# Strassen's scheme for the output products of the last four blocks of an attention and mixture kernel

## The chip, the cores and the metric

The kernel runs on one core of a Trainium2 chip. Such a core has a matrix engine (TensorE, PE in the profile; its weight loads stand apart as PEld), a vector engine (VectorE, DVE), an engine for activations and copies (ScalarE, ACT), a general engine (GpSimd, POOL) and an engine that only issues transfers (SyncE, SP). Each works through its own instructions in order and waits on semaphores for the others. Sixteen DMA engines move data between DRAM and the on-chip memory SBUF; matrix products land in PSUM, eight banks of 512 fp32 values in each of 128 partitions.

The metric is the device time of one execution in microseconds (us).

## The reference

```python
def phi(x):
    proj = np.einsum('bhsd,df->bhsf', x, w_phi)
    proj = proj - np.max(np.abs(proj), axis=-1, keepdims=True)
    return np.concatenate([np.exp(proj), np.exp(-proj)], axis=-1)
q_p, k_p = (phi(q), phi(k))
kv = np.einsum('bhsf,bhsd->bhfd', k_p, v)
z = np.sum(k_p, axis=2)
attn = np.einsum('bhsf,bhfd->bhsd', q_p, kv) / (np.einsum('bhsf,bhf->bhs', q_p, z)[..., None] + 1e-06)
x = attn.transpose(0, 2, 1, 3).reshape(4608, 512)
gate = 1.0 / (1.0 + np.exp(-(x @ w_gate)))      # w_gate, w_val: 512 x 1536
return gate * (x @ w_val) @ w_out               # w_out: 1536 x 512
```

There are 8 batches, 8 heads, 576 positions, 64 features a head, 128 random features, and all values are fp32. This document is about the second half, the gated product of 4608 tokens.

## The kernel before

**Arithmetic.** A factor is split into a high part in the matrix engine's own fp32 form and a low part (the rest), and one product of a 128x128 block takes three matmuls: high by high, high by low, low by high. A matmul loads a 128x128 weight block and streams up to 512 columns past it.

**Blocks.** The 1536 hidden features are twelve blocks j of 128. The first four (j = 0 to 3) are computed during attention, in 9 chunks of 512 tokens, straightforwardly (`gate`, L914; `first_js`, whose output product is `mm_out`, L971); their part of the result goes to DRAM as `ys`. The last eight are four pairs: pairs 0 and 1 (j = 4 to 7) in a first pass over all tokens, pairs 2 and 3 (j = 8 to 11) in a second. Both passes are `pass_over` (L1294), and they run over 6 chunks `dc` of 768 tokens, two halves of 384 each.

**One chunk of a pass.** `x_blocks` (L1149) fetches the four blocks of x (features by tokens) from DRAM, makes the four sums T1 to T4 of Strassen's scheme, and splits each of the seven factors that the scheme uses (`XB`: 11, T2, T3, T1, 21, T4, 22) into high and low (ACT L1187, DVE L1191). `group` (L1216) makes one 256x768 product with seven block products instead of eight: 7 x 2 x 3 = 42 matmuls of 384 columns (L1229), and five additions on DVE (L1242). There are four groups a chunk: gate and value of each of two pairs. `gated` takes the sigmoid on ACT (L1267); `valued` multiplies (DVE L1280), copies the high part (ACT L1284) and subtracts for the low part (DVE L1288). Then the output product: for each of the chunk's six blocks T of 128 tokens, the hidden values are the weights and w_out streams past, 2 pairs x 2 blocks x 3 = 12 matmuls of 512 columns (L1311). `finish` (L1129) fetches the sum so far (L1134), adds it on DVE (L1139) and stores the new sum (L1143): the first pass reads `ys` and writes `yt`, the second reads `yt` and writes `out`.

**Weights.** `combine` (L1054) makes the seven Strassen sums of the weights of one pair's gate (m = 0) or value (m = 1); those of pairs 2 and 3 are made during the first pass and kept in DRAM (`gscr`), and so are the w_out blocks (`out_weight`, `wscr`), a chunk's worth at a time, in the first four chunks. `fetched` (L1111) brings them back.

**Order.** Nothing is ordered by hand. `Plan.run` (L179) is a list scheduler at build time: every operation has an engine, an estimated duration and a rank, and the engine takes, of what can start, the lowest rank; what it finds is the program's order on each engine, which does not change on the chip. Buffers are slots of rings (`Buf`, `Slot`); an operation whose ring is full is not ready. In the passes PE's groups have banks `r_a` (5) and the output products `r_g` (3); x has 14 slots `r_X`, exactly one chunk's; h has 8 slots `r_h`; the y that come back have 3 (`r_y1`). All transfers of the loop are issued by SP, in order.

Of the kernel before, what the change touches and what calls it, by code (L numbers as in the profile page):

```python
# [59 lines left out]
KEEP = 30.0  # L60

# [87 lines left out]
class Plan:  # L149
# [3 lines left out]
    NEAR = {"PE": 0.3, "DVE": 0.05, "ACT": 0.05, "SP": 0.0, "X": 0.0}  # L153
    SAME = {"PE": 0.0, "DVE": 0.12, "ACT": 0.13, "SP": 0.0, "X": 0.0}
    RATE = 0.26
# [23 lines left out]
    def run(self):  # L179
        free = dict.fromkeys(self.NEAR, 0.0)  # L180
        ready = {e: [] for e in free}
        mode, wire = None, 0.0
# [30 lines left out]
        while left:  # L213
# [24 lines left out]
            if o.eng == "SP":  # L238
                wire = max(wire, t) + o.lag * self.RATE ** -1 * 1e-6
                end = wire + 2.0  # L240
            else:
                end = t + o.busy + o.lag
            if o.eng == "PE":
                mode = o.mode[-1]
            for cells in o.opens:
                n = len(cells.free)
                cells.free, cells.taken = [end] * n, [False] * n
# [5 lines left out]
            for n in o.then:  # L253
                n.wait -= 1
                if n.eng != o.eng or o.eng == "SP":
                    at = end + n.slack
                else:
                    at = t + o.busy + self.SAME[o.eng]
# [9 lines left out]
def attention_moe(  # L268
# [18 lines left out]
    actx = ExitStack()  # L287
# [13 lines left out]
    def arena(where, name, size, dtype):  # L301
# [9 lines left out]
        return lambda start=0: Area(view, cells, start * 1024 // CELL)  # L311
# [11 lines left out]
    for hd in range(2):  # L323
# [5 lines left out]
    yscr = [dram.tile([4, P, DM], F32, tag=f"ys{c}", name=f"ys{c}") for c in range(NCH)]  # L329
    y2scr = [dram.tile([4, P, DM], F32, tag=f"yt{c}", name=f"yt{c}") for c in range(NCH)]  # L330
    wscr = [dram.tile([2, P, DM], F32, tag=f"wo{j}", name=f"wo{j}") for j in range(NJ)]
# [3 lines left out]
        for m in range(2)  # L335
# [6 lines left out]
    flat, more = arena(ff, "flat", 32 << 10, F32), arena("two", "more", FB, F32)  # L342
# [14 lines left out]
    r_wo = x.ring(8, DM)  # L357
    x = high()
    r_G = x.ring(8, 7 * 2 * P)
    r_stage = x.ring(2, 7 * 2 * P)  # L360
    r_swo = high(56).ring(7, DM)
    r_x7 = high(42).ring(2 * NC4, CW)
    r_sum = flat(20).ring(1, 2 * DM)
    r_tmp = flat(24).ring(1, 2 * HT)
    r_f = flat().ring(5, HT)
    x = more()
    r_tmp += x.ring(2, 2 * HT)
    r_f += x.ring(6, HT)
# [410 lines left out]
    def weigh(j, m, r, deep, wh, wl, ms, part, after=()):  # L779
        raw = Buf([r_raw], [P, 2 * DM])  # L780
        top = Buf([r_top], [P, DM])
# [185 lines left out]
    def mm_out(acc, t, hs, j, first, last):  # L967
        (hh, hl), (wh, wl) = hs, weights[j][1]
        ts = slice(t * P, t * P + P)
        for i, (a, w) in enumerate(((hh, wh), (hh, wl), (hl, wh))):  # L970
            nc.tensor.matmul(  # L971
                acc(), a()[:, ts], w(), start=first and i == 0, stop=last and i == 2
            )

    def first_js(c, r, step):
# [5 lines left out]
        for t in range(CW // P):  # L981
            acc, y = Buf(banks, [P, DM]), Buf([r_y], [P, DM])

            def go(t=t, acc=acc):
# [15 lines left out]
                256 << 10, lambda t=t, y=y: nc.sync.dma_start(yscr[c][t], y()),  # L1000
# [33 lines left out]
    def swap():  # L1034
        actx.close()
        stage["two"] = ctx.enter_context(tc.tile_pool(name="two", bufs=1, side="right"))

    last = plan.op("X", 0.0, 0.0, swap, after=closing)
    last.opens = [a().cells for a in (high, more)]
    for cells in last.opens:  # L1040
# [5 lines left out]
    names = ["11", "12", "S3", "22", "S1", "S2", "S4"]  # L1046
# [7 lines left out]
    def combine(n, m, r, rings, after):  # L1054
# [7 lines left out]
        for i, j in enumerate(pair(n)):  # L1062
            weigh(
                j, m, r + 3 * i, False, gh, gl,
                slice(2 * i * KH, 2 * (i + 1) * KH), i, after + combined[-1:],
# [8 lines left out]
            )  # L1074
        for o, a, b, op in (
            (3, 2, 3, ALU.add),
            (2, 0, 2, ALU.subtract),
            (0, 3, 0, ALU.subtract),
            (1, 1, 0, ALU.subtract),
# [8 lines left out]
        for o, i, part in ((4, 3, 2), (2, 2, 1), (5, 0, 3), (6, 1, 4)):  # L1088
# [35 lines left out]
    def out_weight(j, r, rings, after):  # L1124
        wh, wl = Buf(rings, [P, DM]), Buf(rings, [P, DM])
        weigh(j, 2, r, False, wh, wl, slice(0, DM), None, after)
        return wh, wl

    def finish(T, acc, src, mark, dst, dmark, r):  # L1129

        c, t = divmod(T, CW // P)
        y1, y = Buf([r_y1], [P, DM]), Buf([r_y], [P, DM])
        sp(
            256 << 10, lambda: nc.sync.dma_start(y1().bitcast(F32), src[c][t]),  # L1134
            [(mark[c], t)], [y1], r - 12.0, [done],
        )
        dve(
            DM,
            lambda: vec.tensor_tensor(y(), acc(), y1().bitcast(F32), op=ALU.add),  # L1139
            [acc, y1], [y], -90.0,  # L1140
        )
        sp(
            256 << 10, lambda: nc.sync.dma_start(dst(c, t), y()), [y],  # L1143
            [(dmark[c], t)] if dmark else [], r,
        )

    prior, taken, outs = [fed], [], []

    def x_blocks(dc, r):  # L1149

        at_ = {n: (Buf([r_X], [P, 2, HT]), Buf([r_X], [P, 2, HT])) for n in XB}
        tmp = [Buf([r_tmp], [P, 2, HT]) for _ in range(3)]
# [6 lines left out]
        def fetch(x, K, h):  # L1159
            t, e = dc * DC + h * HT, dc * DC + h * HT + HT  # L1160
            s = 0
            while t < e:
                c, o = divmod(t, CW)
                wd = min(CW - o, e - t)
# [6 lines left out]
                    [xmark[c]], [x], rank(), prior[-1:],  # L1171
                )
                t, s = t + wd, s + wd
# [10 lines left out]
        def split(n, src):  # L1184
# [10 lines left out]
            )  # L1195

# [19 lines left out]
    def group(weight, x, r):  # L1216

        gh, gl = weight
        a, b, c, d = (Buf([r_a], [P, CW]) for _ in range(4))
        t1, t2, t3 = (Buf([r_f], [P, HT]) for _ in range(3))  # L1220

        def product(o, i, w, xn, first, last):
            k, (xh, xl) = names.index(w) * KH, x[xn]

            def go():
                for cc in range(2):
                    ws = slice(k + cc * P, k + cc * P + P)
# [193 lines left out]
```

## Time and profile before

| what | value |
|---|---|
| median of 3 runs | 1159.23 us (1158.13 to 1159.84) |
| profiled execution, its own time | 1160.85 us |
| its span, first to last instruction | 1158.9 us |
| granted TensorE clock, mean | 0.998 |
| DRAM traffic | 120.06 MB read, 49.42 MB written |
| first matmul of the passes | 598.3 us after the span's start |
| last matmul of the passes ends | 1155.2 us |

The profile is of one execution, about 1.6 us over the median. "Busy" of an engine is the time in which an instruction of it stands in the trace; matmuls are pipelined and overlap, so a busy PE alone does not say that it runs at its pace: the number of matmuls in a stretch does. The chain of waits is followed back from the last instruction, and in order of time it shows, for every stretch, what was on it and how many. In the rows of groups the pair after the bar is total busy time in us and the mean in ns; behind the second bar stands how long the engine had been idle before these instructions.

### The profile page before, as it was taken

What the parts mean: (1) busy time and instruction counts of PE and PEld (TensorE: products, weight loads), DVE (VectorE), ACT (ScalarE), POOL (GpSimd) and SP (SyncE); (2) the same over time, 40 slices, a digit from 0 to 9 for tenths busy, and PEclk for the clock granted to TensorE, in tenths of its full rate; (3) what the DMA queues carried; (4) which work ended last, traced back from release to release, by engine and by line L of the source; (5) the groups of instructions that cost most, each with busy time, mean ns of one, the idle gap of its engine ahead of it and who ended that gap; (6) DMA issues with size and microseconds to landing.
All of it is one profiled execution on the core that took longest, in us unless ns stands there. A gap on an engine that the chain in (4) does not pass through costs nothing.

```text
span 1158.9 us, 22323 instructions
## 1 busy us (share of the span) xinstructions
PE 1142.8 (99%) x8796; PEld 939.5 (81%) x8796; DVE 933.3 (81%) x1793; ACT 583.0 (50%) x1115; POOL 0.7 (0%) x6
## 2 busy tenths in 40 slices
PE   8999999999999999999999999999999999999998
PEld 6666566766676677678889999999999999999997
DVE  6999989888878878847897999988767757757764
ACT  6867776666656666635553444352332333323421
POOL 0000000000000000000000000000000000000000
PEclk9999999999999999999999999999999999999999
DMA  6764554344424443226526656545447433225122
GB/s 237 226 220 127 152 168 123 121 129 137 137 87 153 121 137 122 70 79 209 173 101 211 206 178 223 187 141 186 154 173 286 141 106 123 78 88 163 56 95 82
DMA packets 99441, 171.08 MB, mean 148 GB/s; under 512 B 18825, under 2 KB 43529, under 8 KB 99337
## 3 DMA queue, kind: packets, MB, share of 16 engines
q1 hardware_dynamic: 99336, 169.66, 45.7%
q8 instruction: 69, 1.13, 0.4%
q14 instruction: 36, 0.29, 0.1%
HBM read 120.06 MB, written 49.42 MB: 146 GB/s over the span
## 4 chain that ended last, share of the span: by engine, by line
PE 84%; DVE 7%; DMA 6%; ACT 2%; issue 1%; SPq 1%; DVEq 0%
PE bank L1229 30%; PE gate L1311 17%; PE gate L914 11%; PE gate L971 6%; PE bank L621 4%; PE bank L663 3%; PE bank L914 3%; DMA rb<-den 3%; PE bank L432 2%; PE bank L681 2%; DMA den<-dn 2%; PE bank L537 1%; DVE d L587 1%; PE bank L971 1%; PE bank L635 1%; PE bank L647 1%
## 5 line engine op out<-in xcount | busy, mean ns | idle before, releaser
L1229 PE MATMUL bank<-low,high 128*128 128x384 f32 x2016 | 351.8, 336 | 0.0
L1229 PEld LDWEIGHTS bank<-low,high 128*128 128x128 f32 x2016 | 349.8, 188 | 1.1
L1311 PE MATMUL gate<-low 128*128 128x512 f32 x864 | 198.4, 389 | 0.0
L1311 PEld LDWEIGHTS gate<-low 128*128 128x128 f32 x864 | 162.0, 188 | 33.2
L914 PE MATMUL gate<-low 128*128 128x512 f32 x696 | 165.7, 393 | 1.2 <-ACT flat L949 0.6
L914 PEld LDWEIGHTS gate<-low 128*128 128x128 f32 x696 | 128.6, 188 | 29.7 <-issue 1.2
L479 ACT ACTIVATE ek<-ek 128x512 f32<-128x512 f32 (+1 forms) x192 | 96.6, 526 | 27.3 <-DVE ek L467 25.9
L1242 DVE TENSOR_TENSOR more<-more,bank 128x384 f32<-128x384 f32 x111 | 61.1, 551 | 40.8 <-PE bank L1229 40.3
L971 PE MATMUL gate<-low 128*128 128x512 f32 x384 | 92.3, 394 | 0.0
L971 PEld LDWEIGHTS gate<-low 128*128 128x128 f32 x384 | 70.8, 188 | 15.1 <-issue 1.0
L621 PE MATMUL bank<-ek,vin 128*32 128x256 f32 x1240 | 74.5, 386 | 4.4 <-ACT d L545 3.8
L621 PEld LDWEIGHTS bank<-ek,vin 128*32 128x32 f32 x1240 | 37.8, 110 | 46.2 <-issue 11.0
L1139 DVE TENSOR_TENSOR flat<-gate,low 128x512 f32<-128x512 f32 x72 | 49.3, 685 | 23.3 <-PE gate L1311 11.7
L438 DVE TENSOR_REDUCE mk<-bank 128x4 f32<-128x512 f32 (+1 forms) x92 | 49.0, 552 | 21.3 <-PE bank L432 16.9
L1242 DVE TENSOR_TENSOR flat<-flat,bank 128x384 f32<-128x384 f32 x75 | 41.3, 551 | 29.3 <-PE bank L1229 29.1
L1187 ACT CAST low<-more 128x768 fp32r<-128x768 f32 x36 | 30.1, 836 | 61.1 <-DVE more L1178 60.8
L467 DVE TENSOR_TENSOR ek<-bank,mk 128x512 f32<-128x512 f32 (+1 forms) x92 | 48.2, 550 | 0.6 <-ACT d L550 0.2
L1267 ACT ACTIVATE more<-more 128x384 f32<-128x384 f32 x38 | 20.0, 525 | 57.1 <-DVE more L1242 56.9
L938 ACT CAST low<-flat 128x512 fp32r<-128x512 f32 x36 | 22.3, 620 | 51.5 <-DVE flat L963 44.9
L1284 ACT CAST low<-more 128x384 fp32r<-128x384 f32 x50 | 24.7, 513 | 46.6 <-DVE more L1280 46.6
L590 ACT ACTIVATE eq<-d 128x1152 f32<-128x1152 f32 x29 | 33.9, 1168 | 24.8 <-DVE d L587 24.4
L432 PE MATMUL bank<-wk,kin 64*128 64x128 f32 x496 | 38.7, 289 | 4.6 <-DMA kin<-k 4.3
(184 smaller groups left out, 1700.1 us busy)
## 6 DMA issues: line engine op xcount, KB each, us to landing
flat<-w_moe SPq DMA_DIRECT2D x36, 512.0 KB
low<-xs SPq DMA_DIRECT2D x46, 256.0 KB
kin<-k SPq DMA_DIRECT2D x32, 320.0 KB
qin<-q SPq DMA_DIRECT2D x32, 320.0 KB
vin<-v SPq DMA_DIRECT2D x32, 320.0 KB
ys<-flat SPq DMA_DIRECT2D x36, 256.0 KB
low<-ys SPq DMA_DIRECT2D x36, 256.0 KB
yt<-flat SPq DMA_DIRECT2D x36, 256.0 KB
```

The lines of the kernel that those rows point to most:

```text
L432: nc.tensor.matmul(pk[hd]()[:, t, :], x()[head(hd), t * P : t * P + P], wk[head(hd), :], start=True, stop=True,)
L438: vec.tensor_reduce(mx, pk, axis=AX.X, op=ALU.max, apply_absolute_value=True)
L467: vec.tensor_tensor(ek[g]()[:, :, F:], src, mk[g]()[:, :ns].unsqueeze(2).broadcast_to([P, ns, F]), op=ALU.subtract,)
L479: lambda g=g, sg=sg: act.activation(ek[g]()[:, :, sg * F : sg * F + F], ek[g]()[:, :, F:], AF.Exp, scale=1.0 - 2.0 * sg,),
L621: nc.tensor.matmul(o_[o : o + Q, : 2 * F], vx()[:, 2 * t + hd, o % D : o % D + Q], (e0, e1)[hd][:, t, :] if t < 4 else e2[:, 0, :], start= ...
L663: nc.tensor.matmul(nm()[o : o + Q, :], w()[:, sg, o : o + Q], es[sg]()[:, o // D, cs], start=sg == 0, stop=sg == 1, tile_position=(0, o),)
L914: nc.tensor.matmul(o(), a()[:, ws], x(), start=cc + n == 0, stop=cc == NC4 - 1 and n == 2,)
L971: nc.tensor.matmul(acc(), a()[:, ts], w(), start=first and i == 0, stop=last and i == 2)
L1139: lambda: vec.tensor_tensor(y(), acc(), y1().bitcast(F32), op=ALU.add),
L1229: nc.tensor.matmul(o()[:, :HT], s()[:, ws], y()[:, cc, :], start=first and cc + i_ == 0, stop=cc + i_ == 3, skip_group_check=not first,)
L1242: lambda: vec.tensor_tensor(o(), p(), q()[:, :HT], op=ALU.add),
L1311: nc.tensor.matmul(acc(), s()[:, h, o : o + P], w(), start=i + e + k_ == 0, stop=i + e + k_ == 4,)
```

## The change

Five things are done together, for the two passes only.

1. **Outputs turned.** The output products give output features by tokens: w_out is now the weight and the hidden values stream (`mm_out`, `first_pass`). The kernel's result is 512 x 4608, and the host turns it; `ys` is laid out like x. In the first pass an output is 4 feature blocks x 2 token halves, each 12 matmuls of 384 columns. The first pass adds its result straight into `out`.
2. **Strassen for the output products of the second pass.** `combine` is also run for m = 2 (w_out of a pair), in the last two chunks of the first pass, in place of `out_weight`. `values` makes the seven Strassen sums of the hidden values (four subtractions), in two wide buffers, and splits them. `sent` is a group whose seven products sum over both pairs: 7 x 2 x 3 = 42 matmuls of 384 columns, twice a chunk (m = 0, 1).
3. **Sums of x kept.** The first pass stores T1 to T4, both parts, in DRAM (`tscr`; 8 stores of 384 KB a chunk, not for the last chunk, which is the first of the second pass and stays in SBUF). The second pass fetches them.
4. **Results added by accumulating transfers.** In the second pass GpSimd issues four transfers a `sent` that add to `out` in DRAM; only the last `sent` fetches, adds on DVE and stores through SP.
5. **Order and room.** The second pass takes chunk 5 first, then 0 to 4; the second half of chunk 5's first-pass outputs is put off into the second pass; gates of the next chunk stand between the two `sent` of a chunk; all eight banks serve both. `raw`, `top` and the weight sums of `combine` move to a region that is opened when attention ends, and that region later holds hidden sums (`third`). The planner's transfer rate is 0.36 instead of 0.26 after attention.

The diff, cut to its core:

```diff
-    def mm_out(acc, t, hs, j, first, last):
+    def mm_out(acc, m, hs, j, first, last):
...
-        for i, (a, w) in enumerate(((hh, wh), (hh, wl), (hl, wh))):
+        for i, (w, a) in enumerate(((wh, hh), (wh, hl), (wl, hh))):
             nc.tensor.matmul(
-                acc(), a()[:, ts], w(), start=first and i == 0, stop=last and i == 2
+                acc(), w()[:, ms], a(), start=first and i == 0, stop=last and i == 2
             )
...
+            if n in kinds and dc < NDC - 1:
+                for i, x in enumerate(at_[n]):
+                    k = 2 * kinds.index(n) + i
+                    sp(
+                        384 << 10, lambda k=k, x=x: nc.sync.dma_start(kept_x(k), flat_x(x)),
+                        [x], [(tmark[dc], k)], r + 8.0,
+                    )
...
+        if again:
+            for n in XB:
+                if n in kinds:
+                    for i, x in enumerate(at_[n]):
+                        k = 2 * kinds.index(n) + i
+                        sp(
+                            384 << 10,
+                            lambda k=k, x=x: nc.sync.dma_start(flat_x(x), kept_x(k)),
+                            [(tmark[dc], k)], [x], rank(), prior[-1:],
+                        )
+                else:
+                    fetch(at_[n][1], int(n[0]) - 1, int(n[1]) - 1)
+                    split(n, at_[n][1])
...
-    def group(weight, x, r):
+    def group(terms, r, banks, temps, names=names[0], plus=None):
...
+            for n, (weight, part) in enumerate(terms):
...
+                o_ = pe(
+                    "f", 1.05 / len(terms), go, [*weight, *bufs], [o],
+                    r + 1.04 * (i + n / len(terms)), 0.3, taken[-1:],
+                )
...
+    def first_pass(dc, r):
...
+        for T in range(2 * NC4):
+            acc = Buf([r_g], [P, CW])
+            h, m = divmod(T, NC4)
+            ro = r + 29.2 + 2.1 * T + (SPAN if h and dc == NDC - 1 else 0.0)
...
+    def values(n, x, v, r, banks, after):
+
+        g = group(on_x(ws[n, 1], x), r, banks, r_f2)
+        for i, src in zip((1, 3, 0, 2), g):
+            dve(
+                HT,
+                lambda i=i, src=src: vec.tensor_tensor(
+                    v()[:, i, :], v()[:, i, :], src()[:, :HT], op=ALU.mult
+                ),
+                [src], [(v, i)], -100.0,
+            )
...
+        less(of(t, 0), of(v, 2), of(v, 1), [(v, 2), (v, 1)], [t])
+        less(of(v, 2), of(v, 3), of(v, 2), [(v, 3)], [(v, 2)])
+        less(of(t, 1), of(v, 3), of(t, 0), [(v, 3)], [t])
+        less(of(t, 2), of(v, 0), of(t, 1), [(v, 0)], [t])
+        at_ = {}
+        for src, rings, width, kinds_ in (
+            (v, r_hA, 4, ("21", "11", "T3", "22")),
+            (t, r_hB, 3, ("T1", "T2", "T4")),
+        ):
+            hh, hl = (Buf([rings], [P, width, HT]) for _ in range(2))
+            on_act(
+                width * HT, lambda hh=hh, src=src: act.copy(hh(), src()), [src], [hh], -95.0,
+                after,
+            )
+            dve(
+                width * HT,
+                lambda hh=hh, hl=hl, src=src: vec.tensor_tensor(
+                    hl(), src(), hh().bitcast(F32), op=ALU.subtract
+                ),
+                [src, hh], [hl], -95.0, after=after,
+            )
...
+    def sent(ns, hs, dc, m, r, last=False):
...
+        a, t2, t3, t1 = group(
+            on_h([ws[n, 2] for n in ns], hs, m), r, both, r_f2, names[2], ys
+        )
...
+                plan.op(
+                    "POOL", 0.9, 192 << 10,
+                    lambda f=f, h=h, t=t: nc.gpsimd.dma_start(
+                        final(f, dc, h), t(), accum_op=ALU.add
+                    ),
+                    [t], to, r,
+                )
...
+    for n, dc in enumerate(turns):
+        banks, wait = (both, 0.0) if n else ([r_a], 8.4)
+        hs = [values(2, xb, gv, r, banks, [stored])]
+        gv = gates(3, xb, r + 7.3, banks)
+        hs.append(values(3, xb, gv, r + 14.6, banks, [summed]))
+        if n:
+            sent(ns, hs, dc, 0, r + 21.9)
+        if n < NDC - 1:
+            xb = x_blocks(turns[n + 1], r + 29.2 + wait - XLEAD, True)
+            gv = gates(2, xb, r + 29.2 + wait, both)
+        if not n:
+            r += 15.7
+            sent(ns, hs, dc, 0, r + 21.9)
+        sent(ns, hs, dc, 1, r + 36.5, n == NDC - 1)
+        r += PASS
```

More of the change, by code (lines that the diff above doesn't have):

```diff
@@ L334, in attention_moe @@
         for n in range(2, 4)
-        for m in range(2)
+        for m in range(3)
     }
@@ L341, in attention_moe @@
     low, high = arena(ff, "low", RA, F32R), arena("two", "high", RB, F32R)
-    flat, more = arena(ff, "flat", 32 << 10, F32), arena("two", "more", FB, F32)
+    flat, more = arena(ff, "flat", 32 << 10, F32), arena("prep", "more", FB, F32)
+    third = arena("three", "third", FB, F32R)
     x = low()
@@ L357, in attention_moe @@
     r_wo = x.ring(8, DM)
+    r_hA = low(48).ring(4, 4 * HT)
+    r_hB = low(42).ring(1, 3 * HT) + third().ring(3, 3 * HT)
+    r_O = low(72).ring(2, 7 * 2 * P)
     x = high()
@@ L777, in attend, with weigh @@
             t += wd
-    def weigh(j, m, r, deep, wh, wl, ms, part, after=()):
-        raw = Buf([r_raw], [P, 2 * DM])
-        top = Buf([r_top], [P, DM])
+    def weigh(j, m, r, deep, wh, wl, ms, part, after=(), again=False):
+        raw = Buf([r_raw2 if again else r_raw], [P, 2 * DM])
+        top = Buf([r_top2 if again else r_top], [P, DM])
         def words(x):
@@ L1151, in x_blocks @@
+    prior, taken, outs, sums = [fed], [], [], []
+    omark, tmark = ([Buf() for _ in range(NDC)] for _ in range(2))
+    kinds = ("T1", "T2", "T3", "T4")
+    def x_blocks(dc, r, again):
         at_ = {n: (Buf([r_X], [P, 2, HT]), Buf([r_X], [P, 2, HT])) for n in XB}
-        tmp = [Buf([r_tmp], [P, 2, HT]) for _ in range(3)]
+        tmp = [] if again else [Buf([r_tmp], [P, 2, HT]) for _ in range(3)]
         n_, since = [0.0], len(plan.ops)
@@ L1159, in fetch @@
         def fetch(x, K, h):
[L1160 to L1164, printed above, removed]
+            for c, o, s, wd in pieces(dc, h):
                 sp(
@@ L1251, in group @@
         add(t2, t1, c)
+        first = t1
+        if plus:
+            for o, p, q in ((t2, t2, plus[1]), (plus[2], t1, plus[2]), (t1, t1, plus[3])):
+                add(o, p, q)
+            first = plus[2]
         product(d, 3, "S1", "T1", True, False)
@@ L1327, in attention_moe, with gates @@
-    SPAN = 46.0
-    y2mark = [Buf() for _ in range(NCH)]
+            finish(m, dc, h, acc, ro)
+        return x
+    both = [r_a, r_g]
+    def gates(n, x, r, banks):
+        g = group(on_x(ws[n, 0], x), r, banks, r_f2)
+        v = Buf([r_V], [P, 4, HT])
+        for i, src in zip((1, 3, 0, 2), g):
+            on_act(
+                HT,
+                lambda i=i, src=src: act.activation(v()[:, i, :], src()[:, :HT], AF.Sigmoid),
+                [src], [(v, i)], -100.0, exps,
+            )
+        return v
@@ L1353, in attention_moe, with swap_again @@
+    stored = plan.op("X", 0.0, 0.0, lambda: None, after=plan.ops[-2:])
+    summed = plan.op("X", 0.0, 0.0, lambda: None, after=[stored, *sums])
+    def swap_again():
+        pctx.close()
+        stage["three"] = ctx.enter_context(tc.tile_pool(name="three", bufs=1, side="right"))
+    plan.op("X", 0.0, 0.0, swap_again, after=[stored]).opens = [third().cells]
     start += SPAN * NDC
-    for n, m, late in ((2, 0, []), (2, 1, taken[-4:-3]), (3, 0, outs[-8:-7]), (3, 1, outs[-1:])):
+    for n, m, late in (
+        (2, 0, []), (2, 1, taken[-4:-3]), (3, 0, outs[-12:-11]), (3, 1, outs[-12:-11]),
+    ):
@@ L1355, in attention_moe @@
         ws[n, m] = fetched([r_G], 7 * KH, gscr[n, m], marks[n, m], start, late)
-    for j in (*pair(2), *pair(3)):
-        wo[j] = fetched([r_wo], DM, wscr[j], marks[j], start + 10.0)
-    for dc in range(NDC):
-        pass_over((2, 3), dc, start + SPAN * dc, ws, wo, y2scr, y2mark, final, None)
+    for n in (2, 3):
+        ws[n, 2] = fetched([r_O], 7 * KH, gscr[n, 2], marks[n, 2], start + 20.0, [stored])
+    ns = 2, 3
+    turns = [NDC - 1, *range(NDC - 1)]
+    r = start + 7.3
+    gv = gates(2, xb, start, [r_a])
```

255 lines of the change are left out of this document (165 added, 90 removed).

## The prediction

> **What bounds the kernel now.** I began with the page: busy times, then the chain that ended last by engine.
>
> ```profile
> PE 1142.8 (99%) x8796; PEld 939.5 (81%) x8796; DVE 933.3 (81%) x1793; ACT 583.0 (50%) x1115; POOL 0.7 (0%) x6
> ...
> PE 84%; DVE 7%; DMA 6%; ACT 2%; issue 1%; SPq 1%; DVEq 0%
> ```
>
> PE stands busy nearly always and carries the chain. A busy PE need not run at its pace, so the next view is the chain in order of time (start, length, what, how many) over the second pass.
>
> ```profile
> 886.50 24.96 PE bank L1229 x144
> 911.46 16.36 PE gate L1311 x72
> 927.82 29.12 PE bank L1229 x168
> ...
> 1109.73 29.12 PE bank L1229 x168
> 1138.86 16.37 PE gate L1311 x72
> 1155.23 0.02 issue
> 1155.25 0.69 DVE flat L1139
> ```
>
> Every chunk has the same two lengths to a hundredth: 168 group products in 29.12 us, 72 output products in 16.36 us, nothing between. So PE waits for nothing here. A 384-column matmul takes 29.12/168 = 0.1733 us from start to start, a 512-column one 16.36/72 = 0.2272 us. That is 0.451 against 0.444 ns a column: a fixed part of some 0.012 us stands on each. In these passes a matmul less is time less, and any wait of PE is time more.
>
> Third, the same chunks by windows (busy of PE, PEld, DVE, ACT, POOL with instructions, clock, DMA share, GB/s): two of the first pass, one of the second, then two short stretches in which transfers crowd.
>
> ```profile
> 654.70:700.20 45.50, 45.50 (x241) 42.64 (x240) 44.97 (x87) 21.10 (x39) 0.00 (x0) 1.00 0.65 216
> ...
> 791.20:836.70 45.50, 45.50 (x242) 42.66 (x241) 36.92 (x66) 16.27 (x31) 0.00 (x0) 1.00 0.46 156
> ...
> 911.40:956.90 45.50, 45.50 (x242) 42.66 (x241) 31.97 (x54) 15.57 (x28) 0.00 (x0) 1.00 0.34 105
> ```
> ```profile
> 890.00:895.00 5.00, 5.00 (x30) 5.00 (x29) 2.49 (x6) 0.92 (x3) 0.00 (x0) 1.00 1.02 404
> 895.00:900.00 5.00, 5.00 (x30) 5.00 (x30) 4.37 (x10) 2.28 (x5) 0.00 (x0) 1.00 1.02 341
> ```
>
> DVE is nearly full in the first pass (combining weights) and has room in the second. Full DMA engines move 341 to 404 GB/s; the second pass uses 105.
>
> **PE's own time.** First pass: 72 x 512 columns become 96 x 384. 96 x 0.1733 = 16.64 for 16.36 us, +0.28 a chunk, **+1.7** for six. Second pass: 84 x 0.1733 = 14.56 for 16.36 us, -1.80 a chunk, **-10.8** for six. Net **-9.1 us**. The products of `mm_out` keep shape and count: 0. The form (128x128 weights, 384 columns) is that of L1229, so its pace is measured, and in the all-384 stretches above PEld is already at 5.00 of 5.00, so a saturated load row is within that pace.
>
> The Trainium skill ("TensorE: Matmul & The Clock Gate", section "Wait — 56ns, not 53.3ns?") gives a warm matmul N / 2.4 GHz and some 2.5 ns. By it 384 columns take 0.1625 and 512 0.2158 us, and the change would be worth 504 x 0.1625 + 576 x 0.1625 - 864 x 0.2158 = -11.0 us. The rows show a fixed part five times that, so the narrower matmuls keep less; the sum goes by the rows.
>
> **What is off PE.** Durations of the new shapes come from these groups (busy us, mean ns, idle before):
>
> ```profile
> L1242 DVE TENSOR_TENSOR more<-more,bank 128x384 f32<-128x384 f32 x111 | 61.1, 551 | 40.8 <-PE bank L1229 40.3
> ...
> L1139 DVE TENSOR_TENSOR flat<-gate,low 128x512 f32<-128x512 f32 x72 | 49.3, 685 | 23.3 <-PE gate L1311 11.7 <-DMA out<-flat 9.5 <-DMA yt<-flat 1.6
> ...
> L587 DVE TENSOR_TENSOR d<-d,mb 128x1152 f32<-128x1152 f32 x29 | 39.1, 1348 | 0.0
> ...
> L1191 DVE TENSOR_TENSOR low<-low 128x768 fp32r<-128x768 f32 x36 | 34.2, 950 | 0.1
> ...
> L1187 ACT CAST low<-more 128x768 fp32r<-128x768 f32 x36 | 30.1, 836 | 61.1 <-DVE more L1178 60.8
> ...
> L1288 DVE TENSOR_TENSOR low<-more,low 128x384 fp32r<-128x384 f32 x50 | 27.7, 554 | 5.1 <-ACT low L1284 4.0
> ...
> L1284 ACT CAST low<-more 128x384 fp32r<-128x384 f32 x50 | 24.7, 513 | 46.6 <-DVE more L1280 46.6
> ```
>
> DVE takes 0.398 us for each 384 columns more (950 to 1348 ns), ACT 0.323 (513 to 836). An estimate for 1536 columns is then 1.75 on DVE and 1.48 on ACT.
>
> *DVE, second pass, a chunk:* two groups more, 10 x 0.55 = +5.5; eight subtractions, +4.4; low parts 2 x (1.75 + 1.35) for 8 x 0.55, +1.8; x needs three splits for four sums and seven splits, -8 x 0.95 = -7.6; no `finish`, -6 x 0.685 = -4.1. Together 0: about 32 of 43.7 us. *DVE, first pass:* `out_weight` goes (six instructions of 0.42 to 0.69, -3.3), `finish` is 8 x 0.55 for 6 x 0.685 (+0.3), but combining runs in all six chunks, not four: 42 to 45 of 45.8 us throughout. PE covers it, as in the first chunk quoted; the last combined weights may come 10 us into the second pass, and are wanted 37 us in. ACT stays near 15 us a chunk. All at 0 while PE's products cover it; without that cover DVE's excess over 45.8 us would show directly.
>
> *Hidden sums, the new wait.* After the last value product of pair 3 (call its end V) stand in a row: one addition, one multiplication, two subtractions (4 x 0.55), ACT's wide copy (1.48), DVE's wide subtraction (1.75), with four hand-overs of some 0.1 to 0.2: about 6.0 us. `sent` comes next on PE in rank. Without pair 3 it can do the pair 2 half of four products, 4 x 3 x 0.1733 = 2.08 us. In the four middle chunks the next chunk's gates (42 x 0.1733 = 7.28 us) can stand in the hole: 9.4 against 6.0, hidden; I take 0.25 a chunk for hand-overs, +1.0 (0 to 15.7, if that filler fails: 4 x (6.0 - 2.08)). The last chunk has no next gates; it has both `sent`, 4.16 us of halves, against 6.0: **+1.9** (0 to 6.0). Behind PE's waiting product is everything on PE, and DVE behind it.
>
> *Between the passes* the same chain has one group as filler, and pair 3's w_out sums go where w_out lay, so they are fetched only after the put-off outputs: 1.84 MB at 341 to 404 GB/s is 4.5 to 5.4 us, and up to 3 us latency (the last store below, 2.96). Cover: 7.28 + 2.08 = 9.4. It fits narrowly: +1.0 (0 to 7.3, if the gates are not there).
>
> *Transfers of x.* The second pass fetches 11 x 384 KB = 4.33 MB a chunk instead of four blocks, into slots that the last group frees from V - 6.2 on. At 341 GB/s that is 12.7 us; with 2.3 us latency and the last split (0.84 + 0.95) the last block is ready at V + 10.6. PE, filling 14.6 us with gates and `sent`, wants it at V + 13.5. Cover holds down to 4.33 MB / 15.6 us = 277 GB/s. SP waits there for PE, as now:
>
> ```profile
> SPq L1167 <- PE bank L1229: 90.8, 11, 20.9
> ```
>
> and behind it queue only this x, since the results leave through POOL.
> *First pass:* stores of T1 to T4 add 3.15 MB a chunk, `out_weight` takes 1.05 away: 216 + 2.1 MB / 45.5 us = 262 GB/s, below 341. 0, with the rival below.
>
> *Accumulating transfers.* The page shows POOL with 6 instructions and no transfer of the loop. 44 transfers of 192 KB; the nearest row is a plain 256 KB store by SP at the end: DVE ends at 1155.94, the span at 1158.9, so 2.96 us. Between that and twice that (reading the target too), 3 to 6 us, I take 4. They hold temporaries of a ring of nine: two `sent` take eight, the next group's first the ninth, and its second must find one of the earlier eight free again, some 10 us after the first `sent` ended. Nothing is late until a transfer holds its buffer that long: 0 (up to 5 a chunk beyond it).
> The Trainium skill ("DMA: Bandwidth & Descriptors", "Anatomy of one DMA — SWDGE (gpsimd) path") puts a GpSimd transfer at 2.0 us and bytes / 436 GB/s, an estimate of 2.45 us here, accumulation not counted. That lies under what I took; no row of this trace shows it.
>
> *Ends.* After the last product 0.55 for 0.69 on DVE and 64 KB less: -0.3. At the front, `combine` can fetch raw weights only once attention's room is free; they are needed when the first groups start, and until then old products fill PE. 0, or up to 5 us if that filler ran out.
>
> **Sum.** -9.1 + 1.0 + 1.9 + 1.0 - 0.3 = -5.5. The profiled execution took 1160.85 us (span 1158.9 and 1.95 around it): 1155.3. The median shown is 1159.23: **1153.7 us**. About 0.2% (2.3 us) is what a measurement can tell from no change: 1156.9 to 1161.5 counts as the same.
>
> **Rivals.**
> *The hole stays open (slower).* Each middle chunk's gates wait for x, so the chain of 6.0 us stands bare after 2.08 us of halves. Wholly: 15.7 + 1.9 + 4 at the turn - 9.4 = +12.2, 1171.4; with half of the middle holes (7.85) +4.4, 1163.6. It decides from 277 GB/s downwards, or where the release-to-landing time grows by 3 us. For it: x has exactly one chunk's slots, and fetch, split, group and chain meet in 15 us. Against it: mean traffic there would be (4.33 + 1.57 to 3.1 MB) / 43.7 us = 135 to 170 GB/s. Chance 0.17.
> *First pass pays for the stores.* The old results come back into three buffers, now wanted every 2.08 us instead of 2.73, with stores of 1 us each (384 KB at 400 GB/s) ahead in the same engines. One output in eight late by 1 us is 6 us: 1159 to 1160, the same. For it: 262 GB/s mean, in bursts. Against it: no wait at 216. Chance 0.12.
> *Transfers of POOL hold buffers or SBUF over 10 us.* 1157 to 1165. Chance 0.05, both halves alike.
> *The change does less than it says* would be a 384-column output at more than 0.1733 us; L1229 excludes it.
>
> **Chances.** Forecast, 1149.8 (no waits) to 1156.9: 0.66. With a little of the rivals on either side: faster 0.67, same 0.15, slower 0.18. The range reaches from no waits to half the open holes: 1149.8 to 1163.6.
>
> **What would show it.** Right: in the chain, 96 first-pass outputs in 16.64 us, 42 products of a `sent` in 7.28, and chunks of the second pass 43.7 us apart; PE idle only after the last values (about 2 us) and at the turn. Wrong: gaps before `sent` in each chunk released by DVE or ACT (hole), by a transfer of x (supply); first-pass chunks longer than 45.8 us (stores); additions waiting for POOL's transfers.

## The result, and the profile after

The changed kernel took **1169.36 us** (median of 9 runs, 1163.14 to 1172.34), the kernel before 1159.99 us on the same chips (9 runs): ratio **1.0067, 95% interval 1.0044 to 1.009**. It is slower by 9.4 us where 5.5 less were forecast, and lies above the range. The profiled execution, the longest of the nine, took 1172.34 us (span 1170.5), 17.0 more than the 1155.3 that the sum gave for such an execution.

The page of the changed kernel, busy times and the chain by engine:

```profile
PE 1142.5 (98%) x9012; PEld 966.3 (83%) x9012; DVE 951.3 (81%) x1826; ACT 585.6 (50%) x1095; POOL 39.2 (3%) x50
...
PE 47%; issue 19%; DVE 16%; DMA 9%; ACT 4%; POOL 3%; SPq 1%; DVEq 0%; POOLq 0%; ACTq 0%
```

PE's busy time is what it was (it is a model, and hides pace), yet PE's share of the chain fell from 84% to 47%. Part of that is only the view's: over most of the second pass the chain follows GpSimd's queue (POOL and "issue", pieces of up to 31.87 us), while PE was busy for 257.61 of 259 us. In order of time the chain shows that the products themselves run at the forecast pace:

```profile
791.91 13.54 PE gate L1407 x78
...
888.84 29.12 PE bank L1286 x168
917.96 7.30 PE gate L1407 x42
925.26 1.06 PE bank L1286 x6
```

78 output matmuls of the first pass in 13.54 us are 0.1736 us each; a `sent` takes 7.3 us. The third view counts matmuls in a stretch (us, busy of PE, PEld, DVE, ACT, POOL with instructions, clock, DMA share, GB/s):

```profile
600.00:880.00 280.00, 273.11 (x1538) 268.02 (x1537) 245.21 (x462) 115.17 (x216) 0.00 (x0) 0.99 0.67 233
...
889.00:1148.00 259.00, 257.61 (x1476) 255.60 (x1475) 183.47 (x303) 83.46 (x129) 34.95 (x40) 1.00 0.57 144
...
1145.00:1166.00 21.00, 18.35 (x102) 17.14 (x101) 15.18 (x25) 3.97 (x5) 3.53 (x4) 1.00 0.31 47
```

The yardsticks: the first experiment below has the same products in the same order without first-pass waits, and holds 1598 in 600 to 880. So 60 are missing here, 60 x 0.1733 = 10.4 us; a wait of 1.55 us at the window's start (602.8 to 604.3) belongs to the front. The second pass has one shape; 259 us hold 1494 and 21 us hold 121. Missing are 18 (3.1 us) and 19 (3.3 us).

Without the front, the first pass is the stretch from the first to the last of its 576 output matmuls; of the changed kernel, then of the first experiment:

```profile
L1407 PE MATMUL gate<-low x576: 333/334/444, 642.6 to 927.0; 128*128 128x384 f32 x192
```
```profile
L1407 PE MATMUL gate<-low x576: 334/334/372, 638.3 to 914.3; 128*128 128x384 f32 x192
```

That is 284.4 us for 276.0: the first pass pays **8.4 us**.

*Where the first pass loses it.* Waits of DVE and PE in 598 to 889 (total us, times, longest), then the chain through its first output stretch:

```profile
DVE flat L1168 <- DMA low<-ys: 8.5, 9, 1.9
...
PE bank L1286 <- DVE flat L1305: 5.3, 5, 2.2
```
```profile
652.73 4.20 DMA low<-ys
...
660.02 0.43 SPq L1161
...
660.50 5.14 DMA low<-ys
...
665.74 0.10 DVE flat L1168
...
666.62 0.47 DVE flat L1305
...
667.23 4.93 PE bank L1286 x18
```

An old result, at most 192 KB, is fetched (`low<-ys`) and lands 5.14 us later. DVE's next instruction is the addition that wants it (L1168, `finish`), and DVE works in order, so a group's addition (L1305) stands behind it; that addition would have freed a bank, and PE starts again at 667.23 after 2.24 us. The windows say what the transfers met:

```profile
645.00:650.00 5.00, 5.00 (x30) 4.81 (x28) 4.82 (x10) 3.41 (x7) 0.00 (x0) 1.00 0.20 79
650.00:655.00 5.00, 5.00 (x29) 4.87 (x29) 5.00 (x9) 0.51 (x2) 0.00 (x0) 1.00 0.93 311
655.00:660.00 5.00, 5.00 (x31) 5.00 (x30) 4.58 (x7) 0.82 (x1) 0.00 (x0) 1.00 0.94 330
660.00:665.00 5.00, 4.99 (x29) 4.67 (x27) 3.60 (x8) 1.21 (x3) 0.00 (x0) 1.00 0.90 303
...
680.00:685.00 5.00, 5.00 (x31) 5.00 (x30) 4.80 (x11) 2.82 (x6) 0.00 (x0) 1.00 0.01 2
```

Fetches of old results, stores of sums and stores of T go through SP's one queue in 650 to 665, at shares of 0.90 to 0.94; twenty us later the DMA engines do nothing. The pass's mean of 233 GB/s tells neither.

*The second pass.* Waits of ACT in 889 to 1150 and of PE from 1140 on, and the chain at the end:

```profile
ACT low L1213 <- DMA low<-xs: 22.7, 10, 8.3
```
```profile
PE bank L1286 <- DVE low L1474: 1.4, 1, 1.4
PE bank L1286 <- DVE flat L1305: 1.3, 1, 1.3
```
```profile
1158.63 0.76 POOL out L1516
1159.39 6.69 DMA out<-flat
```

The first PE wait is the last chunk's chain of hidden sums. The second was not forecast. It has two parts: the last `sent` adds the old results on DVE, which its groups' other additions stand behind, and these want temporaries that the last accumulating transfers still hold (the one of 6.69 us is followed by such an addition, L1305). With plain transfers (run 2) this wait is 0.6 us.

The buffers are fewer than they look. The old results of the last `sent` are fetched into the same ring of nine (`ys`, L1486), and since SP takes what can start, all four fetches (`flat<-out`) are issued between 848.8 and 859.0, still in the first pass. The transfers issued in 598 to 889 list them:

```profile
flat<-out SPq DMA_DIRECT2D x4, 192.0 KB
```

The planner gives a buffer back after its last reading, here that of the last sum past 1162. So for the whole second pass groups and accumulating transfers share five temporaries, not nine. No run here puts these fetches off.

*The front.* In 525 to 535 DVE was full before (combining weights) and is half empty now, probably because raw weights are fetched only once attention's room is free; PE's gap follows at 590 to 605. No run tests that link, and the repeat of the changed kernel has no such gap. The first row is of before, the others of the changed kernel:

```profile
525.00:535.00 10.00, 10.00 (x46) 8.21 (x45) 9.87 (x21) 6.37 (x14) 0.00 (x0) 1.00 0.89 285
```
```profile
525.00:535.00 10.00, 10.00 (x45) 8.25 (x44) 4.96 (x8) 4.00 (x8) 0.00 (x0) 1.00 0.77 256
...
590.00:605.00 15.00, 13.45 (x64) 11.34 (x63) 14.93 (x27) 9.74 (x18) 0.00 (x0) 1.00 0.42 142
```

### The profile page after: what moved, and what is told of

Read it like the earlier page. It is cut to its first block, busy times and chain, and to the rows that moved or that the text cites. A ratio compares the mean times of both kernels' runs of the same rounds, so it can differ in the third digit from the quotient of the medians.

```text
span 1170.5 us, 22971 instructions
## 1 busy us (share of the span) xinstructions
PE 1142.5 (98%) x9012; PEld 966.3 (83%) x9012; DVE 951.3 (81%) x1826; ACT 585.6 (50%) x1095; POOL 39.2 (3%) x50
## 4 chain that ended last, share of the span: by engine, by line
PE 47%; issue 19%; DVE 16%; DMA 9%; ACT 4%; POOL 3%; SPq 1%; DVEq 0%; POOLq 0%; ACTq 0%
PE bank L1286 15%; PE gate L925 11%; PE gate L1407 4%; PE bank L632 4%; PE bank L674 3%; POOL out L1516 3%; PE gate L982 2%; DMA low<-ys 2%; DMA rb<-den 2%; DMA more<-w_moe 2%; PE bank L443 2%; PE bank L692 1%; DMA low<-xs 1%; PE bank L646 1%; DVE d L598 1%
## 5 line engine op out<-in xcount | busy, mean ns | idle before, releaser
L1286 PE MATMUL bank<-low,high 128*128 128x384 f32 x1785 | 326.9, 338 | 8.8 <-DVE flat L1305 6.6
L1286 PEld LDWEIGHTS bank<-low,high 128*128 128x128 f32 x1785 | 311.3, 189 | 13.0 <-issue 4.3
L1305 DVE TENSOR_TENSOR flat<-flat,bank 128x384 f32<-128x384 f32 x241 | 131.6, 549 | 64.0 <-PE bank L1286 51.3
L925 PE MATMUL gate<-low 128*128 128x512 f32 x696 | 165.7, 394 | 1.2 <-ACT flat L960 0.6
L925 PEld LDWEIGHTS gate<-low 128*128 128x128 f32 x696 | 128.6, 188 | 29.8 <-issue 1.2
L1407 PE MATMUL gate<-low 128*128 128x384 f32 x576 | 102.5, 335 | 0.0
L1407 PEld LDWEIGHTS gate<-low 128*128 128x128 f32 x576 | 100.3, 188 | 0.3 <-DVE flat L1168 0.3
L982 PE MATMUL gate<-low 128*128 128x512 f32 x384 | 92.3, 394 | 0.0
L982 PEld LDWEIGHTS gate<-low 128*128 128x128 f32 x384 | 70.8, 188 | 15.1 <-issue 1.0
L1516 POOL DMA_DIRECT2D out<-flat x44 | 38.5, 950 | 1121.8 <-DVE flat L1305 994.2
L1286 PE MATMUL gate<-low,high 128*128 128x384 f32 x375 | 74.7, 336 | 0.8 <-ACT flat L1311 0.8
L1286 PEld LDWEIGHTS gate<-low,high 128*128 128x128 f32 x375 | 65.8, 188 | 1.1 <-ACT flat L1311 1.1
L1311 ACT COPY flat<-bank 128x384 f32<-128x384 f32 x47 | 22.3, 475 | 66.7 <-PE bank L1286 66.2
L1305 DVE TENSOR_TENSOR flat<-flat,gate 128x384 f32<-128x384 f32 x59 | 32.4, 552 | 22.5 <-PE gate L1286 17.1
```

The source lines that it names most:

```text
L925: nc.tensor.matmul(o(), a()[:, ws], x(), start=cc + n == 0, stop=cc == NC4 - 1 and n == 2,)
L982: nc.tensor.matmul(acc(), w()[:, ms], a(), start=first and i == 0, stop=last and i == 2)
L1286: nc.tensor.matmul(o()[:, :HT], s()[:, ws], y(), start=first and n + cc + i_ == 0, stop=end, skip_group_check=not first,)
L1305: lambda: vec.tensor_tensor(o(), p(), q()[:, :HT], op=ALU.add),
L1407: nc.tensor.matmul(acc()[:, :HT], w()[:, m * P : m * P + P], s()[:, h, :], start=i + e + k_ == 0, stop=i + e + k_ == 4,)
L1516: lambda f=f, h=h, t=t: nc.gpsimd.dma_start(final(f, dc, h), t(), accum_op=ALU.add),
```

## The experiments

Theory: the first pass pays for crowded transfers, the second for x and for the chain of hidden sums. Rivals: the old results' buffers are too few; the accumulating transfers hold things up; or the order, planned at build time, counts on landings that the chip does not give. Ratios are to the kernel before on the same chip, with 95% intervals. The matmul columns are of one profile each; the first also counts waits of the front up to 604.

| run | median us (n) | ratio | matmuls 600:880 | matmuls 889:1148 |
|---|---|---|---|---|
| the change | 1169.36 (9) | 1.0067 (1.0044 to 1.009) | 1538 | 1476 |
| again | 1168.36 (6) | 1.0076 (1.005 to 1.0101) | 1543 | 1461 |
| 1 no T stores | 1166.44 (4) | 1.0055 (1.0036 to 1.0074) | 1598 | 1428 |
| 2 plain stores | 1165.55 (5) | 1.0061 (1.004 to 1.0083) | 1575 | 1457 |
| 3 T stores later | 1160.34 (10) | 1.0005 (0.9993 to 1.0017) | 1596 | 1458 |
| 4 four buffers | 1166.76 (5) | 1.007 (1.0043 to 1.0097) | 1577 | 1450 |
| 5 no fetch of x | 1157.99 (10) | 0.9977 (0.9967 to 0.9987) | 1584 | 1480 |
| 6 sums split finely | 1157.6 (10) | 0.9974 (0.9962 to 0.9986) | 1589 | 1473 |
| 7 and later landings | **1155.49 (5)** | **0.9962 (0.995 to 0.9975)** | 1595 | 1486 |
| 8 2.5 us, four buffers | 1157.56 (11) | 0.9973 (0.9962 to 0.9985) | 1588 | 1476 |
| 10 as 7, T stores early | 1158.5 (10) | 0.9982 (0.9967 to 0.9998) | 1583 | 1491 |

**1. T is not stored.** The order of all else is the change's; the fetches of T read the same number of bytes from rows of x.

```diff
-  384 << 10, lambda k=k, x=x: nc.sync.dma_start(kept_x(k), flat_x(x)),
+  384 << 10, lambda: None,
...
-            return tscr[dc][k]
+            return xscr[k].rearrange("p a b -> p (a b)")[:, :DC]
```

> The changed kernel with its program order kept and only the 40 stores of T1 to T4 in the first pass left out; the second pass fetches as many bytes in rows of the same length from x instead, so the second pass computes with other sums. Theory crowding: the stores fill the DMA engines in the output stretches, the old results come late, DVE stands at its first-pass additions and PE behind it. Then DVE's wait for old results falls from 8.5 us to under 2, PE's waits in the first pass from about 9 us to under 2, and the time by 6 to 9 us, to about 1161. Rival order: the old results are asked for too late whatever else moves (three buffers, one output each 2.08 us, up to two transfers each). Then DVE still waits over 6 us there and the time falls by less than 3 us.

Both passes by windows, and DVE's wait for old results in 600 to 888:

```profile
600.00:880.00 280.00, 279.94 (x1598) 277.36 (x1597) 251.04 (x476) 116.57 (x219) 0.00 (x0) 1.00 0.56 190
...
889.00:1148.00 259.00, 250.29 (x1428) 247.13 (x1426) 183.54 (x300) 83.14 (x125) 35.07 (x40) 1.00 0.53 131
```
```profile
DVE flat L1168 <- DMA low<-ys: 0.4, 1, 0.4
```

The first pass is whole again: PE is busy 279.94 of 280 us, DVE's 8.5 us of waiting are 0.4, with three buffers and the same order. The stores cause these waits. But the time fell by only 3 us (1.4 by the ratios, within their intervals), since the second pass now lacks 66 matmuls (11.4 us). ACT waited 27.7 us there for x and its substitutes, 22.7 in the change, and four times PE stood behind ACT. Why the substitute rows landed later is not shown. That confounds the total, and suggests how near the second pass lives to its supply of x.

**2. Results stored without adding** (the sum with the first pass is left out).

```diff
-                        final(f, dc, h), t(), accum_op=ALU.add
+                        final(f, dc, h), t()
```

> The changed kernel with the 44 transfers of GpSimd as plain stores of the same bytes from the same queue (the old result is not added). Theory buffers: an accumulating transfer takes 4.4 us to land where a plain one takes about 3, and DVE's additions wait for its buffers (11.9 us of DVE waits over the kernel, of them one of 1.3 us on PE's path at the end). Then landing falls to about 3 us, DVE's waits for these transfers by more than half and the time by 1.5 to 3 us. Rival: the holes of the second pass come from the chain of hidden sums alone; then the time changes by less than 1 us although landing is shorter.

GpSimd's transfers in the second pass (count, size, median us from issue to landing), of the changed kernel and of this one:

```profile
out<-flat POOLq DMA_DIRECT2D x44, 192.0 KB, 4.4
```
```profile
out<-flat POOLq DMA_DIRECT2D x44, 192.0 KB, 2.1
```

DVE's waits for a free buffer in the second pass (11.9 us over 8 times in the change) are gone, but PE lacks 37 matmuls for 18 (33 in the repeat of the change): DVE's waiting lay beside PE's work, but for 0.7 us at the end (1.3 to 0.6). The time forecast for the theory did not come clear: the ratio went from 1.0067 to 1.0061, within the intervals. The first pass runs the same program here, in an execution of 1163.05 us, and lacks 23, not 60; by its output matmuls it takes 280.1 us, 4.1 over run 1. So that loss varies from execution to execution.

**3. T is stored one group later**, when the output stretch is over; the order is planned anew with it.

```diff
-                        [x], [(tmark[dc], k)], r + 8.0,
+                        [x], [(tmark[dc], k)], r + 24.0, taken[-1:],
...
+            if not i:
+                keeps[dc]()
```

> The changed kernel with the stores of T1 to T4 put off: they are issued after the first group of their own chunk instead of as soon as a sum is split. The same bytes move, but in a stretch in which the DMA engines were 0.01 to 0.6 busy instead of 0.9 and more. Theory crowding: as without the stores, DVE's wait for old results under 3 us, PE's waits in the first pass under 3 us, time 1161 to 1163. Rival total traffic or SP's issue time: the waits move with the stores, PE's waits in the first pass stay over 6 us, time 1166 to 1170.

The same bytes, and no wait in the first pass:

```profile
600.00:880.00 280.00, 280.00 (x1596) 276.93 (x1595) 250.02 (x474) 112.68 (x217) 0.00 (x0) 1.00 0.71 246
```

With 246 GB/s this mean is higher than the change's 233, and PE loses nothing: when the bytes go decides, not how many. The time is 1160.34 us, and the ratio 1.0005 for 1.0067. What remains is the second pass. Its timeline at one middle gap (from run 3 on, lines stand some lines further down: the additions of a group are L1311, the copy that empties its first bank L1317):

```profile
964.56 0.83 ACT L1214 CAST low<-low 128x768 fp32r<-128x768 f32 x1 [2.12 <-DMA low<-xs]
...
965.30 0.47 ACT L1317 COPY flat<-gate 128x384 f32<-128x384 f32 x1
...
965.82 0.80 PE L1292 MATMUL gate<-low,high 128*128 128x384 f32 x3 [0.74 <-ACT flat L1317]
```

ACT's next instruction is a split of x, and x comes 2.12 us after ACT is free for it. Behind it stands a copy (L1317) that would empty a bank, and behind that PE. Neither has to do with x.

**4. Four buffers of 384 columns** for old results, instead of three of 512.

```diff
-    r_y1 = x.ring(3, DM)
+    r_y1 = x.ring(4, HT)
```

> The changed kernel with the old results coming back into four buffers of 384 columns instead of three of 512, in the same room. Theory crowding: a request goes out one output (2.08 us) earlier, while a crowded transfer takes 4.2 to 6.2 us; waits in the first pass fall by a third to a half, time by 2 to 5 us, to about 1166. Rival order: four buffers are what was missing, the waits vanish wholly and the time falls by 7 to 9 us without any store being touched.

The first pass lacks 21 for 60, DVE waits 1.2 us for old results, and the time did not fall: the order is planned anew, and the second pass lacks 44 for 18. Whether the buffers did it is not shown, since run 2 with three of them lacks 23 in the first pass. Neither comes down to the 2 of run 3.

**5. On top of 3, the second pass's x and T are not fetched** (it computes with what lies in SBUF).

```diff
-                    lambda c=c, o=o, s=s, wd=wd: nc.sync.dma_start(
+                    lambda c=c, o=o, s=s, wd=wd: None if again else nc.sync.dma_start(
...
-  lambda k=k, x=x: nc.sync.dma_start(flat_x(x), kept_x(k)),
+  lambda: None,
```

> The kernel with put-off stores, its program order kept, and only the transfers of x and its sums in the second pass left out: the splits and products work on what lies in the buffers. Theory supply: in the middle chunks ACT stands at the split of the last fetched block, and the copy of the next group's first product stands behind it with PE (gaps of 0.9, 0.6, 1.1 and 0.5 us and small ones, some 4 us). Then these go, the two gaps of the last chunk (1.6 and 1.6) stay, and the time falls by 3 to 5 us, to about 1156. Rival chain: PE waits for the hidden sums of pair 3 in every chunk, whatever x does; then the gaps stay and the time changes by less than 1 us.

PE's only waits in the second pass from 889 on are now:

```profile
PE bank L1292 <- DVE low L1482: 1.3, 1, 1.3
PE bank L1292 <- DVE flat L1311: 1.0, 1, 1.0
```

Both lie after 1125: the middle gaps are gone with x, the last chunk's stay. So the middle belongs to x's landing, the end to something else. The time fell by 2.4 us against run 3 (3.2 by the ratios), at the lower end of what was forecast.

**6. On top of 3, the hidden sums are copied and split block by block**, as each is ready: 7 + 7 instructions of 384 columns for 2 + 2 wide ones.

```diff
-                width * HT, lambda hh=hh, src=src: act.copy(hh(), src()), [src], [hh], -95.0,
+                    HT,
+                    lambda hh=hh, src=src, i=i: act.copy(hh()[:, i, :], src()[:, i, :]),
+                    [(src, k)], [(hh, i)], -95.0, after,
```

> The kernel with put-off stores and the hidden sums split block by block (seven copies and seven subtractions of 384 columns in the place of two and two wide ones), so that the first products of the output group wait for one block and not for four. Theory chain: the gap of 1.6 us before the last chunk's output groups goes, time down by 2 to 4 us, to 1156 to 1158. Rival supply: only that one gap goes, the middle gaps stay as they were, and the time falls by less than 2 us. If DVE were the bound, its ten more instructions a chunk would make it slower.

The chain's last stretch, where run 3 had an accumulating transfer of 5.50 us, is now PE alone:

```profile
1148.46 2.10 PE bank L1292 x12
1150.57 1.05 PE gate L1292 x6
...
1151.64 0.56 DVE flat L1311
```

Both gaps of the last chunk are gone. The first came from the chain; that the second went too may be the order, which is planned anew. Middle gaps stay (1473 of 1494): at 969.27 and 1058.18 PE waited 0.73 and 1.08 us, now for DVE, which came to that addition late because ACT had stood at x first.

**7. On top of 6, the planner counts a transfer as landed 3 us (SP) or 4 us (GpSimd) after its bytes**, not 2.0, and ten temporaries serve instead of nine.

```diff
-                end = wire + 2.0
+                end = wire + (2.0 if rate == self.RATE[0] else 3.0 if o.eng == "SP" else 4.0)
...
-    r_f2 = r_f[:5] + flat(8).ring(2, HT) + r_f[8:10]
+    r_f2 = flat().ring(10, HT)
```

> As the one before, with ten buffers for temporaries instead of nine, and the order made with transfers that land 1 us later after attention (3 instead of 2 us after the last byte, 4 for those of GpSimd); what is computed is the same. Theory order: the program's order takes transfers for quicker than they land, and each in-order engine that comes to its wait too early holds up what stands behind it. Then ACT's and DVE's waits for x, old results and accumulating transfers shrink by half or more, PE's waits after attention come below 5 us, and the time is 1151 to 1154, faster than before the change. Rival: what is no longer waited for is given back as work placed later; 1157 to 1160.

```profile
889.00:1148.00 259.00, 258.69 (x1486) 257.95 (x1485) 192.90 (x374) 92.65 (x188) 38.23 (x44) 1.00 0.55 135
```
```profile
ACT low L1214 <- PE bank L1292: 13.3, 4, 3.7
ACT low L1214 <- PE gate L1415: 7.5, 1, 7.5
```

ACT's split of x now waits mostly for PE, which frees the room; its waits for the transfer fell from 22.8 to 6.4 us, the longest from 8.5 to 1.3. PE has 0.5 us of waits left after 600. This version is faster than both kernels, 1155.49 us, though not the 1151 to 1154 that were expected. Its interval overlaps that of run 6; the two profiles agree with a gain (13 matmuls more in the second pass, 2.3 us, for 2.1 us of time). The allowance and the tenth temporary were not tried apart; with four of them held by the old results, the second is six for five.

**8. As 7, with 2.5 us for SP and four buffers.**

```diff
-  else 3.0 if o.eng == "SP" else 4.0)
+  else 2.5 if o.eng == "SP" else 4.0)
...
-    r_y1 = x.ring(3, DM)
+    r_y1 = x.ring(4, HT)
```

> As the one before, with a landing time of 2.5 us in the order and four buffers for the old results. Theory order: between the two kernels before, 1151 to 1155; four buffers help the first pass where the wait for old results is still over 1 us.

No better than 7, and above the range that was expected: 1157.56 us. Two things differ from 7, so the size of the allowance is not settled by this run.

**9. The changed kernel again**, and **10. as 7 with the T stores where the change has them.**

```diff
-                        [x], [(tmark[dc], k)], r + 24.0, taken[-1:],
+                        [x], [(tmark[dc], k)], r + 8.0,
```

> The changed kernel itself once more, for a second profile: the first one was of its slowest run (1172.34 us of 1163.14 to 1172.34). Theory crowding: what differs between its runs is the first pass, whose old results land at different times in crowded stretches; a run of 1165 to 1169 us shows 4 to 7 us of waits there instead of 9, and the same 7 us in the second pass. Rival: the runs differ in attention or in the second pass.

> The best kernel so far (block-wise splits, ten buffers, order made with a landing time of 3 us) but with the stores of T1 to T4 issued as early as in the change. Theory crowding: their place matters by itself, because bytes that are ahead in the same engines delay what PE waits for; DVE's wait for old results comes back with 3 us or more and the time is 1159 to 1163. Rival order: an order that knows of the landing time absorbs it; then 1155 to 1157, the same as with put-off stores.

The profile of the repeat is again of its longest execution (1172.47 of 1164.02 to 1172.47), so it does not say what the shorter ones lack. It has the same two losses (55 matmuls, 9.5 us, in the first pass, 33 or 5.7 us in the second); by the output matmuls the first pass takes 285.3 us, 9.3 over run 1. In run 10 the first pass lacks 15, 2.6 us:

```profile
600.00:880.00 280.00, 278.76 (x1583) 274.61 (x1582) 250.28 (x474) 113.72 (x218) 0.00 (x0) 1.00 0.68 241
```

DVE waits 1.9 us for old results, and the time, 1158.5 us, lies between the theory's range and the rival's. So in this order the early stores cost some 2 us, where in the change they cost 4 to 9. Run 10 has the allowance, the tenth temporary and the finer splits together; the last two act on the second pass's groups, which speaks for the allowance here, but no run has it alone.

## Why the prediction was wrong

*PE's own time, -9.1: right.* The pace is the forecast one, and run 10 holds 1491 of 1494 possible matmuls in 259 us of the second pass.

*"First pass: stores of T1 to T4 add 3.15 MB a chunk ... 262 GB/s, below 341. 0": the step that failed.* The term was 8.4 us in the profile and 9.3 in the repeat's, both of the longest executions; in run 2's, a shorter one with the same first pass, it was 4.1. The added mean came out as reckoned (186 GB/s before, 233 after in 600 to 880, where 46 were added), but a mean over 45.5 us was laid against the limit of a full queue, while the stores, the old results and the sums share the same 15 us at 303 to 330 GB/s. There the landing of an old result was 4.2 to 6.2 us, and an in-order DVE carried that to PE. Runs 1 and 3 show it, one by taking the stores away, one by moving them. The rival had the mechanism at 0.12 and priced it at 6 us; its "no wait at 216" was the same mean again.

*Middle holes, +1.0: 3.1 in the one profile, 5.7 in the other, and by another way.* The forecast looked at the chain of hidden sums and held x to be ready 2.9 us before PE wants it. Run 5 shows that x's landing makes these gaps, through ACT: the sum asked when PE wants x, not what stands behind the split on ACT. The rival "hole open" spoke of gates that wait for x; here a copy that has nothing to do with x waits.

*Last chunk, +1.9: right*, 1.4 us of idle PE, and run 6 removes it. *Ends, -0.3: wrong.* PE stood 1.3 us more at the last `sent`, behind DVE's additions of the old results and the temporaries that transfers still held. The step counted only what follows the last product, and that took 4.1 us for 3.7 before.

*Turn between the passes, +1.0: it cost nothing*; groups and `sent` follow each other without a gap from 888.84 to 926.32.

*Accumulating transfers, 0: nearly, but partly by luck.* A landing of 4.4 us was taken as 4; run 2 gains nothing in the middle of the second pass without the adding, and 0.7 us at the end. The argument counted on nine temporaries where five were left: DVE did wait for transfers, 11.9 us in 8 times, and PE's work mostly covered it. The Trainium skill ("DMA: Bandwidth & Descriptors", "Anatomy of one DMA — SWDGE (gpsimd) path") gives an estimate of 2.45 us for this size; the plain transfers took 2.1, so it is near, and the adding about doubles the landing, which that section does not count.

*Front, 0 or up to 5: between.* In one profile PE lost 0.7 us in 535 to 545 and 1.55 us of 15 in 590 to 605, in that of the repeat 0.06 of the latter (busy 14.94). The first output matmul starts at 642.6 and 639.7 for 638.4 before. No run here moved it by itself.

The sum, by these marks in the profile: the front 4.3 us (642.6 for 638.4), the first pass 8.4, what follows the last product 0.7 more than forecast. The last matmul ends at 1166.4 where the forecast has it at 1155.2 - 5.2 = 1150.0; less front and first pass, 3.7 of these 16.4 are the second pass and the turn. Together 17.1 for the 17.0 us. Of the front, some 2.3 us are waits of PE that the kernel before does not have; what the rest is stays open. The range failed for a further reason: the rivals were taken as if only one could come true, but first pass, holes and front came together, and their prices add.

## What to carry to other kernels

Lay the transfers of a change against the limit stretch by stretch, where they meet what is awaited, not as a mean over a pass. For every awaited transfer ask what stands behind the waiting instruction on its engine, and who waits for that: both losses here reached PE over an instruction that had no use for the late data. Where the order is fixed at build time, let it allow for landings as the trace has them under load. Stores put off (1.0067 to 1.0005), finer hand-overs (0.9974) and such an order with one temporary more (0.9962, not clear of the step before) turned this change from a loss of 0.7% into a gain of 0.4%.

## Not expected of the hardware

*A short wait can lower the clock, and need not.* In both profiles of the change PE had one wait of 2.24 or 2.25 us in the first pass. The windows behind it, of the change and of its repeat:

```profile
667.20:670.60 3.40, 3.37 (x11) 3.40 (x12) 2.24 (x6) 1.43 (x3) 0.00 (x0) 0.55 0.83 232
```
```profile
664.00:667.40 3.40, 3.40 (x11) 3.40 (x12) 2.20 (x6) 1.42 (x3) 0.00 (x0) 0.51 0.74 225
```

For 3.4 us the granted clock was 0.55 and 0.51, and 11 matmuls ran instead of 19.6: 8.6 x 0.1733 = 1.5 us lost on top of 2.24. The Trainium skill ("TensorE: Matmul & The Clock Gate", "What's actually happening") puts the cold state behind at least one idle window of some 3.4 us that runs freely; the length of the slow stretch and its clock agree, but here a wait of 2.24 us was enough. Even 1.64 us can be. In attention, some 163 us in, PE waits 1.63 to 1.64 us in the profile of the change and of every variant. The windows behind it, of the change and of run 3:

```profile
165.80:169.20 3.40, 3.40 (x41) 1.89 (x36) 3.09 (x5) 2.79 (x6) 0.00 (x0) 0.50 0.43 143
```
```profile
164.40:167.80 3.40, 3.40 (x88) 2.46 (x84) 3.14 (x5) 3.20 (x8) 0.00 (x0) 1.00 0.60 144
```

The one ran 41 matmuls at clock 0.50, the other 88 at 1.00. A wait of 2.06 us at the front of run 5 was not followed by a low clock either (16 matmuls in the next 3.4 us, some of 512 columns, at clock 1.00), nor was the longest of run 2's first pass, 1.60 us. So the length of the wait alone does not decide. The 1.5 us are part of the 8.4 that the first pass lost.

*Some issues on SP are slow in the crowded stretches.* SP's own queue in the crowded stretch (start, us, what):

```profile
650.11 0.32 SPq L1161 DMA_DIRECT2D low<-ys  x1
...
652.23 1.56 SPq L1161 DMA_DIRECT2D low<-ys  x2
...
656.90 2.03 SPq L1161 DMA_DIRECT2D low<-ys  x2
```

Two issues (x2) for old results took 1.56 and 2.03 us together, where one shortly before took 0.32. Over the change's 72 issues the median is 0.44 us and the longest 1.47; in run 1, without the stores of T and with DMA shares of 0.50 and 0.72 in 645 to 655, 0.42 and 0.50. So most issues are not slow, and whether it is the full DMA engines or the stores ahead in the same queue that slow some is not separated. Part of the delay of an old result is thus spent before its transfer is under way.
